# Four first chunks summed on TensorE with two products from GpSimd, one adding transfer per chunk, and a new issue order in a convolution and feed-forward kernel

## The chip, the cores and the metric

The kernel runs on one NeuronCore of one Trainium2 chip. The metric is the device time of one execution in microseconds (us), lower is better. The engines are named as in the profile: PE is TensorE (the matmuls), DVE is VectorE, ACT is ScalarE, POOL is GpSimd, and SP is SyncE, which only issues transfers.

## What is computed

For 8 sequences of 4224 positions with 192 features, each position becomes a weighted sum of itself and its six predecessors (seven taps, a softmax of given scores for each of eight heads). The result goes through a layer norm and a two-layer network with a ReLU, and is added to the network's output.

```python
w = softmax(weight_gen)                      # [8, 4224, 8 heads, 7 taps], over the taps
out = einsum('bshk,bskhg->bshg', w, x_unf)   # x_unf: the seven shifted copies of x
xn = (out - mean(out)) / sqrt(var(out) + 1e-6) * g_ln
y = out + maximum(xn @ w_ch1, 0.0) @ w_ch2   # w_ch1 [192, 768], w_ch2 [768, 192]
```

The inputs `g_ln`, `w_ch1` and `w_ch2` come as 64-bit floats, and the kernel turns them into 32-bit and then pairs of 16-bit floats itself.

## The kernel before

**Tiling.** The 33,792 positions lie as 128 partitions by 264 columns. A *chunk* is 4 or 6 columns of the convolution; a *group* is 4 columns of the network (512 positions), 66 in all. The kernel is recorded as a list of operations (`op`), and the table `PLACE` gives each a number; `order` sorts them by it, so that each engine's instruction order is written out by hand. Engines run their own lists in order and wait on semaphores.

**Convolution** (`conv`). For a chunk, four products are made: taps 1 and 2 as one pair (`c0`), taps 3 and 4 (`c1`), tap 0 alone into the chunk's output `y` (`c2`), taps 5 and 6 (`c3`). A pair goes into one `pr` buffer of two planes; there are five. For ordinary chunks DVE makes all four (line 511). Then POOL issues two transfers that add plane 2 to plane 1 and plane 4 to plane 3 (`dma_add`, line 517), and four adds on POOL (line 514) sum taps 5, 6, 1 and 3 into `y`. The first `DIRECT = 3` chunks, four columns each, go another way: POOL makes taps 5 and 6, DVE the other three products, and PE sums all seven planes into PSUM by matmuls with an identity matrix (`gather`, line 532), from where ACT copies them to `y`.

**Softmax** (`softmax`): DVE and POOL and ACT share its steps; the first transfers of scores and of `x` feed it and the first products.

**Norm** (`norm`): ACT sums and squares each column (lines 564, 569), DVE corrects the root in five small instructions (lines 597 to 603), ACT scales into `xh` (615) and rounds to 16 bits (`hl`, 635), POOL subtracts the rounded value for the low half (`lo`, 648), and SP transposes the two halves by a transfer into `xT` (`turn`, 652). Adding transfers and transposes are kept apart: each waits for the last one of the other kind that was placed ahead of it (`behind` in `order`).

**Network.** A group has three *units* of the first layer (`unit_products`, line 670, 36 matmuls each) into one of two `ph` buffers in PSUM. Each unit's result is taken out by ACT (ReLU to 16 bits, `hh`, line 685) and then by DVE (the low half, `hlo`, line 687); only then is its `ph` buffer free for the unit after next. The second layer of a group is two halves (`half_output`, `p0` and `p1`, line 721, 72 matmuls each), and DVE adds them to `y` (line 773), which SP stores (781). In the recorded loop the two halves of a group stand behind the second and third unit of the next group. `weights` prepares the weight matrices during the first 75 us; the low half of the second layer's weights (`c_w2l`, line 938, POOL) comes last. `wake` (line 642) is 11 matmuls whose result nobody reads.

Of the kernel before, what the change touches and what calls it, by code (L numbers as in the profile page):

```python
# [22 lines left out]
DIRECT = 3  # L23
# [8 lines left out]
    'wload': (3, 9, 33, 42, 82, 86, 121, 257, 191, 373, 568, 527, 770, 1053, 851, 1068, 1156, 1216, 1427, 1301,  # L32
        1465, 1705, 1809),
    'load': (26, 12, 32, 37, 85, 87, 102, 103, 84, 120, 298, 261, 337, 260, 421, 466, 456, 526, 338, 569, 642,
        641, 756, 712, 769, 783, 849, 885, 978, 1067, 979, 1162, 1159, 1163, 1302, 1343, 1368, 1369, 1572, 1426,
        1566, 1569, 1613, 1806, 1768, 1769, 1808, 1938, 1905, 2076, 2134, 2035),
    'w_load': (40, 11, 13, 0, 1, 2),
    'w_load2': (58,),
    'w_as': (67,),
    'w_av': (41, 44, 65, 73),  # L40
    'w_an': (80,),
    'w_cs': (20,),
    'w_cv': (15, 17, 22, 23),
# [223 lines left out]
def kernel(  # L267
# [735 lines left out]
```

## Time and profile before

| | |
|---|---|
| time, median of 3 runs | 868.85 us (868.65 to 870.63) |
| span of the profiled execution (first to last instruction) | 867.2 us |
| median time less that span | 1.65 us |
| PE busy | 823.4 us (95%) |
| DVE busy | 772.1 us (89%) |
| ACT busy | 683.7 us (79%) |
| POOL busy | 679.6 us (78%) |
| first unit of the network starts | 64.04 us |
| last matmul group starts | 856.81 us |

The profiled execution has no time of its own beside its span; the 1.65 us is what the time has around the span in the median of the runs. An engine's busy share is an average over stages. What matters is which engine is waited for in each stage, which the waits and the table by stage tell.

### The profile page before, as it was taken

What the parts mean: (1) busy time and instruction counts of PE and PEld (TensorE: products, weight loads), DVE (VectorE), ACT (ScalarE), POOL (GpSimd) and SP (SyncE); (2) the same over time, 40 slices, a digit from 0 to 9 for tenths busy, and PEclk for the clock granted to TensorE, in tenths of its full rate; (3) what the DMA queues carried; (4) which work ended last, traced back from release to release, by engine and by line L of the source; (5) the groups of instructions that cost most, each with busy time, mean ns of one, the idle gap of its engine ahead of it and who ended that gap; (6) DMA issues with size and microseconds to landing.
All of it is one profiled execution on the core that took longest, in us unless ns stands there. A gap on an engine that the chain in (4) does not pass through costs nothing.

```text
span 867.2 us, 37431 instructions
## 1 busy us (share of the span) xinstructions
PE 823.4 (95%) x16665; PEld 787.7 (91%) x16665; DVE 772.1 (89%) x796; ACT 683.7 (79%) x1781; POOL 679.6 (78%) x390
## 2 busy tenths in 40 slices
PE   3857999999999999999999999999999999999997
PEld 2526999999999999999999999999989999999997
DVE  6899999999999999999999999999989989874442
ACT  2798898799678889889888789787887888796631
POOL 3399999899889999897887889888976788885100
PEclk9968999999999999999999999999999999999999
DMA  7768868988897958988899698878948569565123
GB/s 193 190 127 166 166 163 184 200 176 180 194 193 151 220 94 188 213 181 180 160 205 195 149 213 175 165 139 187 207 99 200 120 151 190 124 127 106 40 76 110
DMA packets 137465, 140.89 MB, mean 162 GB/s; under 512 B 107479, under 2 KB 109015, under 8 KB 137303
## 3 DMA queue, kind: packets, MB, share of 16 engines
q1 hardware_dynamic: 123175, 88.95, 44.9%
q0 software_dynamic: 13824, 49.55, 29.6%
q8 instruction: 130, 2.13, 1.1%
q14 instruction: 32, 0.26, 0.1%
q10 hardware_dynamic: 304, 0.00, 0.0%
HBM read 36.43 MB, written 25.95 MB: 72 GB/s over the span
## 4 chain that ended last, share of the span: by engine, by line
PE 68%; DVE 9%; issue 2%; DVEq 0%
PE ph L670 34%; PE po L721 34%; DVE pr L511 4%; DVE hlo L687 2%; DVE y L511 1%; DVE y L773 1%; PE ph L750 1%; DVE sm L449 0%; DVE mx L440 0%; DVE wn L465 0%; DVE wn L460 0%; DVE wn L461 0%; DVE wn L459 0%; DVE wn L599 0%; DVE wn L601 0%
## 5 line engine op out<-in xcount | busy, mean ns | idle before, releaser
L514 POOL TENSOR_TENSOR y<-y,pr 128x1152 f32<-128x1152 f32 (+1 forms) x192 | 474.5, 2499 | 39.0 <-DVE pr L511 22.1
L670 PE MATMUL ph<-xT,c_w 64*128 64x256 f16 x7128 | 420.0, 270 | 10.5 <-DVE hlo L687 7.8
L670 PEld LDWEIGHTS <-c_w 64*128 64x128 f16 x7128 | 377.6, 94 | 28.3 <-issue 13.5
L721 PE MATMUL po<-c_w2h,hh 64*128 64x192 f16 x3120 | 392.5, 243 | 1.4 <-issue 1.0
L721 PE MATMUL po<-c_w2h,hlo 64*128 64x192 f16 x3120 | 392.4, 243 | 0.5 <-issue 0.5
L721 PE MATMUL po<-c_w2l,hh 64*128 64x192 f16 x3120 | 392.4, 243 | 0.0
L721 PEld LDWEIGHTS <-hh 64*128 64x128 f16 x6240 | 345.7, 94 | 2.8 <-issue 1.9
L511 DVE TENSOR_TENSOR pr<-x,wn 128x2304 f32<-128x2304 f32 (+1 forms) x150 | 332.5, 2226 | 6.6 <-POOL y L514 1.8
L687 DVE SCALAR_TENSOR_TENSOR hlo<-ph,hh 128x1024 f16<-128x1024 f32 x198 | 239.2, 1219 | 57.2 <-ACT hh L685 56.9
L685 ACT ACTIVATE hh<-ph 128x1024 f16<-128x1024 f32 x198 | 200.3, 1015 | 105.2 <-PE ph L670 101.7
L721 PEld LDWEIGHTS <-hlo 64*128 64x128 f16 x3120 | 225.5, 94 | 0.7 <-issue 0.7
L648 POOL TENSOR_TENSOR hl<-xh,hl 128x768 f16<-128x768 f32 x66 | 115.0, 1748 | 44.5 <-ACT hl L635 33.0
L615 ACT ACTIVATE xh<-y,s 128x192 f32<-128x192 f32 x264 | 125.5, 535 | 16.1 <-DVE s L603 12.5
L569 ACT ACTIVATE junk<-y,s 128x192 f32<-128x192 f32 x264 | 119.6, 453 | 6.9
L517 POOL DMA_DIRECT2D pr<-pr x96 | 94.4, 1082 | 37.3 <-DMA xT<-hl 14.2
L564 ACT ACTIVATE junk<-y 128x192 f32<-128x192 f32 x264 | 95.1, 360 | 13.6 <-POOL y L514 7.2
L773 DVE SCALAR_TENSOR_TENSOR y<-po,c_fs,y 128x768 f32<-128x768 f32 (+1 forms) x80 | 67.9, 860 | 5.4 <-PE po L721 5.4
L511 DVE TENSOR_TENSOR y<-x,wn 128x1152 f32<-128x1152 f32 (+1 forms) x51 | 60.0, 1181 | 0.1
L635 ACT ACTIVATE hl<-xh 128x768 f16<-128x768 f32 x66 | 55.0, 837 | 2.1 <-DMA xT<-hl 1.1
L564 ACT ACTIVATION_READ_ACCUMULATOR junk<-y 128x1 f32 x264 | 49.5, 188 | 0.0
L569 ACT ACTIVATION_READ_ACCUMULATOR junk<-y,s 128x1 f32 x264 | 49.4, 187 | 0.0
L532 PE MATMUL ph<-pr,ident 128*128 128x384 f32 x72 | 27.1, 531 | 16.5 <-DVE pr L511 15.6
(76 smaller groups left out, 298.5 us busy)
## 6 DMA issues: line engine op xcount, KB each, us to landing
pr<-pr POOLq DMA_DIRECT2D x60, 576.0 KB, 7.8
x<-in_x_dram SPq DMA_DIRECT2D x30, 576.0 KB, 6.3
out_dram<-y SPq DMA_DIRECT2D x30, 576.0 KB, 5.2
pr<-pr POOLq DMA_DIRECT2D x36, 384.0 KB, 5.8
x<-in_x_dram SPq DMA_DIRECT2D x20, 384.0 KB, 5.5
out_dram<-y SPq DMA_DIRECT2D x20, 384.0 KB, 5.3
w<-in_weight_gen_dram SPq DMA_DIRECT2D x21, 336.0 KB, 5.8
pr<-in_moe_w_ch_dram SPq DMA_DIRECT2D x1, 1152.0 KB
```

Of the source, the lines that this page charges most:

```text
L511: E.tensor_tensor(out=ov, in0=xv, in1=wv, op=ALU.mult)
L514: Q.tensor_tensor(out=flat(0), in0=flat(0), in1=flat(k), op=ALU.add)
L517: return Q.dma_start(flat(to), flat(k), accum_op=ALU.add, max_dma_last_dim=CHUNK * D * 4)
L564: A.activation(junk, at(y)[:, j, :], AF.Identity, scale=-1.0 / D, accum_out=at(s4)[:, 3, t : t + 1])
L569: A.activation(junk, at(y)[:, j, :], AF.Square, bias=at(s4)[:, 3, t : t + 1], accum_out=at(s4)[:, 0, t : t + 1])
L615: A.activation(paired(xh, t), at(y)[:, i, :].rearrange("p (c q) -> p c q", q=P // 2), AF.Identity, bias=at(s4)[:, 3, g + t : g + t + 1], s ...
L648: lambda xh=xh, hl=hl: Q.tensor_tensor(out=halves(hl, True), in0=pairs(xh), in1=halves(hl, False), op=ALU.subtract),
L670: T_.matmul(ph[:, r, v * 2 * P : (v + 1) * 2 * P], W["w1"][rows, WB[r][c], w, f : f + P], xv[rows, a, c, :, :], start=(v == 0 and k == 0), ...
L685: lambda: A.activation(at(hh)[:, us, :], at(ph), AF.Relu), [ph], [(hh, u)])
L687: lambda: V.scalar_tensor_tensor(out=at(hlo)[:, us, :], in0=at(ph), scalar=0.0, in1=at(hh)[:, us, :], op0=ALU.max, op1=ALU.subtract),
L721: made.append(T_.matmul(at(po)[:, z, e * D : (e + 1) * D], token(b, 2 * z + e, j)[rows], W[w][rows, j, :], start=(ph == 0 and e == 0 and k ...
L773: V.scalar_tensor_tensor(out=ysl, in0=at(po)[:, zs[0] : zs[-1] + 1, : 2 * D], scalar=W["fs"][:, 0:1], in1=ysl, op0=ALU.mult, op1=ALU.add)
```

## The change

The first part of four columns is cut into two chunks of two columns, and `DIRECT` is 4, so the same first twelve columns are summed by PE, as four chunks of 2, 2, 4 and 4 columns. For these chunks POOL makes taps 3 and 4 too (`BY_POOL = (3, 5)`). The five two-plane buffers `pr` are replaced by two four-plane buffers `pq` (taps 1 to 4) and two two-plane buffers `pr` (taps 5 and 6). The two adding transfers of an ordinary chunk become one, which adds planes 2 and 4 to planes 1 and 3 when both are there. The helper buffer of the weight preparation moves from `pr` to `xh`. In the recorded loop the second group's three units all stand ahead of the first group's two output halves. And `PLACE` is new as a whole.

```diff
-DIRECT = 3
+DIRECT = 4
+BY_POOL = (3, 5)
...
-    'unit': (209, 210, 224, 228, 232, 249, 264, 279, 288, 302, 304, 328, 341, 342, 369, 379, 388, 406, 423, 426,
+    'unit': (162, 171, 193, 219, 229, 237, 268, 270, 291, 306, 307, 325, 343, 349, 364, 388, 393, 408, 422,
...
-    'p0': (248, 287, 327, 368, 405, 448, 481, 503, 554, 588, 636, 670, 703, 723, 771, 807, 839, 870, 905, 948,
+    'p0': (244, 278, 316, 351, 397, 432, 469, 510, 546, 584, 619, 656, 697, 720, 755, 791, 821, 857, 893,
...
-    pool("pr", 5, [P, 2, CHUNK, D], F32)
+    pool("pq", 2, [P, 4, CHUNK, D], F32)
+    pool("pr", 2, [P, 2, CHUNK, D], F32)
...
-            m = min(CHUNK, n - o) if n % CHUNK == 0 else min(4, n - o)
+            m = 2 if s0 == 0 else min(CHUNK, n - o) if n % CHUNK == 0 else min(4, n - o)
...
-        prs = {k: Buf("pr") for k in (1, 3, 5)}
+        pq, pr = Buf("pq"), Buf("pr")
...
+        def plane(k, nk=1):
+            b, i = (pq, k - 1) if k < 5 else (pr, k - 5)
+            return at(b)[:, i : i + nk, :n, :]
...
-        def dma_add(to, k):
-            return Q.dma_start(flat(to), flat(k), accum_op=ALU.add, max_dma_last_dim=CHUNK * D * 4)
+        def dma_add():
+            a = at(pq).rearrange("p (i j) t d -> p j i (t d)", j=2)[:, :, :, : n * D]
+            return Q.dma_start(a[:, 0], a[:, 1], accum_op=ALU.add, max_dma_last_dim=CHUNK * D * 4)
...
-            if direct and i == 3:
-                op("Pool", q_ns(2 * nd), (f"c{i}", t0), lambda k=k: mul(k, 2, Q), [*xr, (ch["soft"]["e"], "w")], w)
+            if direct and k in BY_POOL:
+                op("Pool", 1.89 * 2 * nd, (f"c{i}", t0), lambda k=k: mul(k, 2, Q), [*xr, (ch["soft"]["e"], "w")], w)
...
-        for i, k in enumerate((1, 3)):
-            op("Pool", 610, (f"d{i}", t0), lambda k=k: dma_add(k, k + 1), [(prs[k], 1)],
-               [(prs[k], 0)], dma=600.0 + 400.0 * n, kind="add")
+        op("Pool", 610, ("d0", t0), dma_add, [tap(2), tap(4)], [tap(1), tap(3)], dma=600.0 + 800.0 * n, kind="add")
...
-        m, t = Buf("pr"), Buf(space)
+        m, t = Buf("xh"), Buf(space)
...
+            late = prev["prev"] is not None and prev["prev"]["prev"] is None
             for u in range(3):
                 products(prev, u)
-                if u and prev["prev"]:
+                if u and prev["prev"] and not late:
                     half_output(prev["prev"], u - 1, prev["s"])
+            if late:
+                for z in range(2):
+                    half_output(prev["prev"], z, prev["s"])
```

The first numbers of `unit` and `p0` show the order on PE: before, five units (209 to 232) stand ahead of the first `p0` (248); now six (162 to 237) stand ahead of it (244).

On DVE, at the first products of the direct chunks (line 511 before, 521 now; `x` times the softmax weights `wn`), before:

```order
L511 TENSOR_TENSOR pr1_77<-x_63,wn0_104 128x2x768
L511 TENSOR_TENSOR y0_67<-x_63,wn0_104 128x768
L459 TENSOR_SCALAR wn0_104<-sm1_97 128x64
L460 TENSOR_TENSOR wn0_104<-wn0_104,rr1_95 128x64
L461 SCALAR_TENSOR_TENSOR wn0_104<-wn0_104,rr1_95 128x64
L511 TENSOR_TENSOR pr2_78<-x_63,wn0_104 128x2x768
L465 TENSOR_TENSOR wn0_104<-e1_99,wn0_104 128x448
L440 TENSOR_REDUCE mx0_92<-w2_66 128x96
L511 TENSOR_TENSOR pr3_79<-x_63,wn0_104 128x2x768
L511 TENSOR_TENSOR y1_68<-x_63,wn0_104 128x768
L511 TENSOR_TENSOR y2_69<-x_63,wn0_104 128x768
L511 TENSOR_TENSOR pr4_80<-x_63,wn0_104 128x2x768
```

and now:

```order
L521 TENSOR_TENSOR pq0_76<-x_63,wn0_103 128x2x384
L462 TENSOR_SCALAR wn0_103<-sm1_96 128x64
L463 TENSOR_TENSOR wn0_103<-wn0_103,rr1_94 128x64
L464 SCALAR_TENSOR_TENSOR wn0_103<-wn0_103,rr1_94 128x64
L847 SCALAR_TENSOR_TENSOR ph0_104<-hh0_87,ph0_104 128x384
L521 TENSOR_TENSOR y0_67<-x_63,wn0_103 128x384
L521 TENSOR_TENSOR pq1_77<-x_63,wn0_103 128x2x384
L850 SCALAR_TENSOR_TENSOR ph0_104<-hh0_87,ph0_104 128x384
L521 TENSOR_TENSOR y1_68<-x_63,wn0_103 128x384
L854 SCALAR_TENSOR_TENSOR hlo0_89<-xh0_80,ph0_104 128x384
L468 TENSOR_TENSOR wn0_103<-e1_98,wn0_103 128x448
L443 TENSOR_REDUCE mx0_91<-w2_66 128x96
```

A direct chunk has one pair product on DVE now instead of two, and the first two chunks have half-size ones; the softmax and weight steps between them stay.

On POOL at the start (442 before and 445 now are the softmax's subtraction, 517 and 528 the adding transfer, 905 and 913 the first layer's low weights, 648 and 656 `lo`), before:

```order
L511 TENSOR_TENSOR pr0_76<-x_63,e0_98 128x2x768
L442 TENSOR_TENSOR e0_98<-w2_66,mx0_92 128x672
L511 TENSOR_TENSOR pr2_78<-x_63,e1_99 128x2x768
L511 TENSOR_TENSOR pr4_80<-x_63,e1_99 128x2x768
L442 TENSOR_TENSOR e0_98<-w0_64,mx1_93 128x672
L442 TENSOR_TENSOR e1_99<-w1_65,mx0_92 128x672
L517 DMA pr3_79<-pr3_79 128x768
L648 TENSOR_TENSOR hl0_83<-xh0_81,hl0_83 128x2x384
```

and now:

```order
L521 TENSOR_TENSOR pr1_79<-x_63,e0_97 128x2x384
L445 TENSOR_TENSOR e0_97<-w2_66,mx0_91 128x672
L521 TENSOR_TENSOR pq0_76<-x_63,e1_98 128x2x768
L521 TENSOR_TENSOR pr0_78<-x_63,e1_98 128x2x768
L445 TENSOR_TENSOR e0_97<-w1_65,mx1_92 128x672
L521 TENSOR_TENSOR pq1_77<-x_63,e1_98 128x2x768
L521 TENSOR_TENSOR pr0_78<-x_63,e1_98 128x2x768
L528 DMA pq0_76<-pq0_76 128x2x768
L445 TENSOR_TENSOR e1_98<-w0_64,mx0_91 128x672
L913 TENSOR_TENSOR c_w1_126<-hlo0_89,c_w1_126 128x768
L913 TENSOR_TENSOR c_w1_126<-hlo0_89,c_w1_126 128x384
L656 TENSOR_TENSOR hl0_82<-xh0_80,hl0_82 128x2x384
```

Three more half-size products stand just ahead of this piece, so POOL makes four products of each size where it made three of full size, and one adding transfer is issued ahead of the first `lo`.

On DVE around the first evictions of the network (`hlo`, line 687 before, 695 now), from the first to the fourth before:

```order
L687 SCALAR_TENSOR_TENSOR hlo0_90<-ph1_106,hh0_88 128x1024
L459 TENSOR_SCALAR wn0_104<-sm0_96 128x96
L460 TENSOR_TENSOR wn0_104<-wn0_104,rr0_94 128x96
L461 SCALAR_TENSOR_TENSOR wn0_104<-wn0_104,rr0_94 128x96
L687 SCALAR_TENSOR_TENSOR hlo0_90<-ph0_105,hh0_88 128x1024
L511 TENSOR_TENSOR pr3_79<-x_63,wn0_104 128x2x768
L687 SCALAR_TENSOR_TENSOR hlo0_90<-ph1_106,hh0_88 128x1024
L440 TENSOR_REDUCE mx1_93<-w1_65 128x96
L511 TENSOR_TENSOR pr1_77<-x_63,wn0_104 128x2x768
L687 SCALAR_TENSOR_TENSOR hlo1_91<-ph0_105,hh1_89 128x1024
```

and from the second to the fourth now:

```order
L695 SCALAR_TENSOR_TENSOR hlo0_89<-ph0_104,hh0_87 128x1024
L521 TENSOR_TENSOR y7_74<-x_63,wn0_103 128x768
L521 TENSOR_TENSOR y8_75<-x_63,wn0_103 128x768
L462 TENSOR_SCALAR wn0_103<-sm0_95 128x96
L463 TENSOR_TENSOR wn0_103<-wn0_103,rr0_93 128x96
L464 SCALAR_TENSOR_TENSOR wn0_103<-wn0_103,rr0_93 128x96
L695 SCALAR_TENSOR_TENSOR hlo0_89<-ph1_105,hh0_87 128x1024
L521 TENSOR_TENSOR pr0_78<-x_63,wn0_103 128x2x768
L695 SCALAR_TENSOR_TENSOR hlo1_90<-ph0_104,hh1_88 128x1024
```

The evictions follow closer on each other. Counted over both orders from the start, what stands ahead of the fourth eviction is five pair products of 1536 elements, two reduces of the softmax and one five-instruction root correction fewer, and two products of 384 elements more.

## Rows read from the trace of the kernel before

**Rows 1.** The page's first part: busy time of each engine, share of the span, and count of instructions.

```profile
PE 823.4 (95%) x16665; PEld 787.7 (91%) x16665; DVE 772.1 (89%) x796; ACT 683.7 (79%) x1781; POOL 679.6 (78%) x390
```

**Rows 2.** The table by stage, four stretches and two finer ones of the start: stretch in us, its length, then busy us and instructions of PE, PEld, DVE, ACT and POOL, the granted clock of PE, the DMA engines' share and GB/s.

```profile
0.00:80.00 80.00, 47.38 (x255) 29.25 (x257) 67.15 (x112) 54.51 (x150) 51.36 (x39) 0.87 0.73 168
80.00:270.00 190.00, 187.38 (x3976) 186.26 (x3972) 187.39 (x195) 160.97 (x436) 174.65 (x113) 1.00 0.84 182
270.00:856.00 586.00, 581.81 (x12360) 565.68 (x12356) 515.19 (x488) 468.21 (x1196) 453.63 (x240) 1.00 0.74 156
...
0.00:20.00 20.00, 6.33 (x11) 3.53 (x12) 12.84 (x25) 4.79 (x12) 7.50 (x11) 1.00 0.77 197
20.00:40.00 20.00, 17.13 (x55) 9.94 (x55) 16.96 (x28) 14.46 (x46) 5.90 (x3) 1.00 0.81 212
70.00:80.00 10.00, 6.34 (x78) 5.31 (x79) 8.32 (x11) 7.43 (x13) 10.00 (x7) 0.66 0.79 156
```

**Rows 3.** The waits of PE from 80 to 270 us and then from 270 to 856 us: who waited for whom, us in total, times, longest.

```profile
PE ph L670 <- DVE hlo L687: 2.6, 6, 1.0
PE po L721 <- DVE y L773: 0.3, 1, 0.3
...
PE ph L670 <- issue: 2.5, 2, 1.4
PE po L721 <- issue: 1.5, 2, 1.0
```

**Rows 4.** The waits of DVE from 0 to 80 us, same columns.

```profile
DVE mx L440 <- DMA w<-in_weight_gen_dram: 2.9, 2, 2.5
DVE pr L511 <- DMA x<-in_x_dram: 1.8, 1, 1.8
DVE hlo L687 <- ACT hh L685: 1.6, 1, 1.6
DVE pr L511 <- PE po L860: 1.4, 1, 1.4
DVE pr L511 <- ACT e L471: 1.1, 1, 1.1
```

**Rows 5.** PE in order of time at the start of the network: start, us, instruction and count, and the idle time before with what ended it.

```profile
59.45 4.66 PE L642 MATMUL ph<-hl 128*128 128x512 f16 x11
64.04 4.10 PE L670 MATMUL ph<-xT,c_w 64*128 64x256 f16 x72
73.35 6.08 PE L670 MATMUL ph<-xT,c_w 64*128 64x256 f16 x72 [5.21 <-DVE hlo L687]
79.75 2.14 PE L670 MATMUL ph<-xT,c_w 64*128 64x256 f16 x36 [0.31 <-DVE hlo L687]
81.71 0.26 PE L721 MATMUL po<-c_w2h,hh 64*128 64x192 f16 x2
```

**Rows 6.** DVE in order of time, single lines of it: three pair products in a row and the next instruction; then a reduce and its successor; and the fourth eviction.

```profile
60.69 5.07 DVE L511 TENSOR_TENSOR pr<-x,wn 128x1536 f32<-128x1536 f32 x3
65.68 0.15 DVE L863 TENSOR_SCALAR c_r<-po 128x1 f32<-128x1 f32 x1
...
68.74 0.17 DVE L597 TENSOR_SCALAR wn<-s 128x4 f32<-128x4 f32 x1
...
69.49 2.67 DVE L511 TENSOR_TENSOR y<-x,wn 128x768 f32<-128x768 f32 x3
...
79.61 0.84 DVE L440 TENSOR_REDUCE mx<-w 128x96 f32<-128x672 f32 x1
80.37 1.75 DVE L511 TENSOR_TENSOR pr<-x,wn 128x1536 f32<-128x1536 f32 x1
82.03 1.22 DVE L687 SCALAR_TENSOR_TENSOR hlo<-ph,hh 128x1024 f16<-128x1024 f32 x1
```

**Rows 7.** Groups by line, kept apart by form, over the whole span: shapes, count, busy us and mean ns of one, idle time before and its releasers.

```profile
L511 DVE TENSOR_TENSOR pr<-x,wn 128x1536 f32<-128x1536 f32 x60 | 104.1, 1746 | 6.0 <-DMA x<-in_x_dram 1.8 <-POOL y L514 1.6 <-PE po L860 1.4
L773 DVE SCALAR_TENSOR_TENSOR y<-po,c_fs,y 128x768 f32<-128x768 f32 x50 | 50.5, 1010 | 3.4 <-PE po L721 3.4
L511 DVE TENSOR_TENSOR y<-x,wn 128x768 f32<-128x768 f32 x21 | 19.6, 946 | 0.0
L773 DVE SCALAR_TENSOR_TENSOR y<-po,c_fs,y 128x384 f32<-128x384 f32 x30 | 17.4, 610 | 2.0 <-PE po L721 2.0
L511 POOL TENSOR_TENSOR pr<-x,e 128x1536 f32<-128x1536 f32 x3 | 8.7, 2904 | 17.5 <-ACT e L471 7.2 <-ACT pr L849 6.0 <-DMA x<-in_x_dram 4.3
L517 POOL DMA_DIRECT2D pr<-pr x96 | 94.4, 1082 | 37.3 <-DMA xT<-hl 14.2 <-DVE pr L511 10.3 <-DVE hlo L687 7.5
```

**Rows 8.** One period of the steady part, from the chain that ended last: start, us, what.

```profile
709.72 1.97 PE ph L670 x36
711.69 2.97 PE po L721 x72
714.66 3.93 PE ph L670 x72
718.59 2.97 PE po L721 x72
721.56 0.47 PE ph L670 x9
```

**Rows 9.** Adding transfers and transposes: the instructions that issue two adding transfers of 576 KB from 332.2 to 333.5 us, with the least, median and greatest time from issue to landing of the two; the same last line for all 66 transposes; and SP's waits over the whole span for the transposes (line 652).

```profile
L517 POOL DMA_DIRECT2D pr<-pr x2: 869/1024/1180, 332.4 to 332.9; - x2
...
DMA to landing us min/median/max: 7.9/9.2/10.5
...
DMA to landing us min/median/max: 3.2/3.7/7.2
...
SPq L652 <- DMA pr<-pr: 166.0, 30, 11.2
```

**Rows 10.** POOL in order of time around the first `lo` and SP's first transposes.

```profile
44.79 1.94 POOL L648 TENSOR_TENSOR hl<-xh,hl 128x768 f16<-128x768 f32 x1
...
56.39 1.60 SPq L652 DMA_TRANSPOSE xT<-hl  x1
```

More of the change, by code (lines that the diff above doesn't have):

```diff
@@ new lines @@
+    'w_load': (16, 2, 0, 32, 28, 24),
+    'w_load2': (72,),
+    'w_as': (88,),
+    'w_av': (76, 82, 86, 94),
+    'w_an': (95,),
+    'w_cs': (45,),
+    'w_cv': (18, 33, 39, 46),
+    'w_cn': (60,),
+    'w_s1': (103, 104, 109, 110, 115),
+    'w_h': (120, 126, 124, 132),
+    'w_l': (129, 135),
+    'w_m': (139, 136, 145, 142),
+    'w_c2s': (105, 160, 181),
+    'w_c2v': (113, 118, 119, 123, 127, 130, 155, 164, 172, 178, 182, 187),
+    'w_c2n': (151, 186, 191),
+    'w_s2': (203, 206, 208, 211, 213, 214, 217, 225),
@@ new lines @@
+    'max': (6, 12, 51, 84, 98, 125, 269, 391, 355, 488, 732, 663, 949, 1118, 861, 1184, 1317, 1291, 1506,
+        1437, 1542, 1710, 1787),
+    'sub': (8, 15, 52, 85, 121, 235, 331, 430, 565, 669, 745, 883, 952, 1126, 1051, 1220, 1338, 1406, 1527,
+        1653, 1781, 1819, 1973),
+    'exp': (11, 20, 56, 92, 153, 248, 378, 442, 604, 676, 777, 894, 1052, 1159, 1060, 1253, 1352, 1412,
+        1552, 1659, 1814, 1843, 1987),
+    'sum': (14, 22, 61, 143, 179, 271, 450, 475, 616, 694, 826, 924, 1072, 1183, 1088, 1282, 1431, 1446,
+        1599, 1799, 1832, 1926, 2083),
@@ new lines @@
+    'rcp': (17, 26, 64, 168, 210, 304, 467, 495, 653, 714, 849, 955, 1101, 1185, 1099, 1306, 1436, 1485,
+        1607, 1803, 1880, 1948, 2089),
+    'inv': (19, 29, 66, 207, 222, 407, 505, 611, 712, 768, 864, 1009, 1115, 1197, 1285, 1339, 1475, 1613,
+        1639, 1808, 1897, 1998, 2103),
+    'mul': (21, 48, 79, 212, 322, 425, 536, 642, 735, 824, 923, 1014, 1119, 1211, 1314, 1401, 1521, 1617,
+        1707, 1809, 1905, 2002, 2106),
+    'keep': (23, 49),
[16 rows of a table added]
+    'copy': (65, 73, 111, 146),
+    'sums': (69, 75, 117, 112, 169, 148, 200, 205, 242, 263, 276, 257, 299, 292, 344, 334, 399, 386, 421,
[7 rows of a table added]
@@ L492, in conv, with tap @@
         yw = [(y, j) for j in range(n)]
+        def plane(k, nk=1):
+            b, i = (pq, k - 1) if k < 5 else (pr, k - 5)
+            return at(b)[:, i : i + nk, :n, :]
+        def tap(k):
+            return (pq, k) if k < 5 else (pr, k)
         def flat(k):
@@ L535, in conv @@
             for i, ks in enumerate(((1, 2), (0,), (3, 4), (5, 6))):
[L536 to L537 removed]
+                op("PE", 160 * n * len(ks), (f"z{i}", t0), lambda ks=ks, i=i: gather(ks, i == 0, i == 3),
+                   [q for k in ks for q in ([tap(k)] if k else yw)], [z], lat=400.0)
             op("ACT", a_ns(nd, 150), ("copy", t0),
@@ L825, in mv @@
         def mv():
-            return at(m)[rows, 0].rearrange("p t d -> p (t d)")[:, :n]
+            return at(m)[rows].rearrange("p t d -> p (t d)")[:, :n]
         def tv(dt):
```

76 lines of the change are left out of this document (20 added, 56 removed), and 235 rows, old and new, of the table PLACE.

## The prediction

> **What bounds the kernel now.** I read the busy shares first: PE leads with 823.4 of 867.2 us, DVE follows with 772.1 [rows 1]. A share mixes stages, so the table by stage comes next [rows 2]. It shows three. Up to 80 us the network barely runs and nothing is full: PE 47.4, DVE 67.2 and POOL 51.4 of 80 us. From 80 to 270 us PE and DVE are both full, 187.38 and 187.39 of 190. From 270 to 856 us PE is full (581.8 of 586) and DVE has room (515.2). The waits say who holds whom [rows 3]: from 80 to 270 us PE waits for DVE alone (evictions of the first layer 2.6 us, an output 0.3); after 270 us it waits for no engine and no transfer, only 4.0 us in four pauses that the profile ascribes to nothing. So from 270 us on the kernel is a fixed amount of matmul work, 11.84 us for each group of four columns (one period: 709.72 to 721.56) [rows 8], and the end moves by what PE is ahead or behind at about 270 us. Until then DVE decides, so the time is won or lost before 80 us, in what DVE has done by then.
>
> **DVE's work: what goes.** The direct chunks lose their taps 3 and 4 on DVE. Before, three chunks of four columns had six pair products of 1536 elements; now two chunks of four have two, and the two of two columns have one half-size pair each (768 elements). A product of 1536 costs 1.746 us, one of 768 0.946 [rows 7]; one of 384 I estimate from these at 0.5. So four of 1536 go (-6.98), two of 768 come and one tap-0 product of 768 goes (+0.95), two tap-0 products of 384 come (+1.0). The first group's output is added in two pieces, since it lies in two `y` buffers: 2 x 0.610 for 1.010 [rows 7], +0.21. Sum: -4.8 us, all of it ahead of 80 us except the last term.
>
> **DVE's idle time.** DVE idles 80 - 67.15 = 12.85 us before 80 us [rows 2]. The waits name some of it [rows 4]: 2.9 for the first scores, 1.8 for the first `x`, 1.6 for an eviction behind ACT, 1.4 behind PE and 1.1 behind ACT. The scores stay first in need and nothing there gets shorter. The first `x` transfer shrinks from 1920 to 1536 elements a partition, and the sums on PE come in smaller pieces, sooner. The last four can win between 0 and 5.9 us; new waits can cost: a chunk's taps 1 to 4 now need one of only two `pq` buffers. A loss as large as the work saved, 4.8, is where I put that end. I take -2.5, a little under half of the 5.9, since each of the four stands before work that the new order brings forward. DVE is then 4.8 + 2.5 = 7.3 us ahead.
>
> **PE's start.** Five units ran before the first output half, which started at 81.71 [rows 5]; the sixth needs the fourth eviction, since there are two `ph` buffers. That eviction started at 82.03 [rows 6]. Ahead of it the new order has five products of 1536 less (start to start (65.68 - 60.69) / 3 = 1.66 each), two reduces less (80.37 - 79.61 = 0.76), one root correction less (69.49 - 68.74 = 0.75) and two products of 384 more (about 0.5): -8.3 - 1.5 - 0.75 + 1.0 = -9.6 [rows 6]. With 2.5 less idle it starts at 82.03 - 9.6 - 2.5 = 69.9 and ends 1.22 later; the sixth unit runs 1.97 [rows 6, 8] to 73.1, and the first half follows. The same six units would have been done at 81.71 + 1.97 = 83.7 before. PE is 10.5 us ahead at that point, more than DVE. In the stretch up to 270 us, where PE waits for DVE, that shrinks towards DVE's 7.3.
>
> **What POOL gets.** Before, three products of 1536 elements at 2.904 us [rows 7]; now four of 768 and four of 1536, together 9216 elements for 4608, so 17.4 us for 8.7. POOL was busy 7.50 + 5.90 of the first 40 us [rows 2], so 26.6 us are free to take 8.7 more. The deadline is the first `lo`: it stood at 44.79 and its transpose left only at 56.39 [rows 10]. The new order puts the first layer's low weights and one adding transfer ahead of it, and even 9 us later it would be no later than the transpose was. I cost it at nothing; if POOL's free time is not where the products are ready, each us beyond that margin is a us on the first unit, not yet on the sixth.
>
> [...]
>
> **Adding transfers.** 96 issues at about 1 us of POOL [rows 7] become 48. POOL is not waited for by PE anywhere [rows 3], so this earns nothing directly. The bytes are the same. A merged transfer of 1152 KB is not in the trace; the nearest rows are a single one of 576 KB (7.9 us to landing) and two issued 0.5 apart, of which the second landed at 332.9 + 10.5 = 343.4, 11.0 after the first issue [rows 9]. I take 11.0, as the same bytes go through the same queue, and keep 7.9 for the lower end.
>
> **The sum.** Against the profiled span: 867.2 - 7.3 = 859.9. With the 1.65 us that the median has around the span: **861.5 us**, 0.8% less than 868.85. PE's work is unchanged: the four direct chunks hold as many columns as the three did.
>
> **Rivals.**
> *PE keeps its lead.* If DVE's order lets PE run through, the gain is 10.5: 858.4. For it: DVE has more to spare in the later groups, and the last long DVE wait was under 1.0 us [rows 3]. Against it: DVE at 187.39 of 190 us [rows 2] cannot catch up 3 us there. What PE's clock does to it: after an idle stretch of 5.21 us the next 72 matmuls took 6.08 for 4.10 before it, at a granted 0.66 in that stretch [rows 2, 5]. PE has three idle stretches now before the first half (ahead of the first, third and fourth unit) for one. [...]
> [...]
>
> *The saved work is idled away.* The two `pq` buffers make DVE wait for PE's sums at the start, or the longer ACT queue ahead of the first ReLUs does. It decides if DVE's idle before 80 us rises by 4.8 or so, to 17.6: then 868.9, no change. For it: the direct chunks pass through two buffers for taps 1 to 4 where they had a choice of five smaller ones. Against it: four chunks are summed on PE with no other matmuls between them.
>
> *The merged transfer holds up the transposes: slower.* Transposes wait for the last adding transfer ahead of them, 30 times and 166 us in total before [rows 9], behind which no PE wait stood [rows 3]. An ordinary chunk of six columns has 1.5 x 11.84 = 17.8 us [rows 8]. Its merged transfer (11.0), one and a half transposes (3.7 each, 5.6) and two hand-overs make about 17, so it fits by less than 1 us. If the merged transfer lands after 13.0 instead of 11.0 on the mean, because loads and stores share the 16 DMA engines, a chunk takes 18.8, 1.0 too long, over the 30 chunks of six columns: +30, less 7.3, gives 891. It decides from about 11.9 us on. Against it: the two adding transfers of a chunk could already stand back to back, as in these rows, so the phases of the two kinds grow little, and before 856 us no unit from 80 us on waited for `xT` [rows 3].
>
> *It does not do what it says* would show as unchanged transfers; the order on POOL shows 48, so no chance is kept for it.
>
> **How the numbers follow.** The forecast (DVE's lead decides, with idle from -5 to +2, so 859 to 866) gets 0.62; PE keeping its lead (858.4 to 860.4) 0.16; the saved work idled away (866.3 to 871.4) 0.11; slower by transfers 0.11. Under about 0.3% (2.6 us) a measurement of this kernel does not tell from no change. So faster 0.78, same 0.11, slower 0.11. The range from 857.0 to 868.5 holds the first two cases and about half of the third's lower part; it leaves out the slower case and a part of the third.
>
> **What would show it.** In the profile after: DVE busy about 767 in all, 4.8 less; DVE idle before 80 us near 10; the first output half of PE near 73 with six units ahead of it; from there to 270 us PE's waits for evictions at least as long as the 2.6 of before, and none after 270; POOL's adding transfers 48, landing in about 11 us for six columns. Wrong would be: PE waiting for the transposed tiles in the steady part (then the transfers decide), DVE idle of 17 us or more by 80 us, or a lead at 270 us that is kept below 4 or above 9.

## The result, and the profile after

The changed kernel takes 880.22 us in the median (874.97 to 882.24, four runs), the kernel before beside it 869.68. The ratio is 1.012, with a 95% interval from 1.0085 to 1.0155: 1.2% slower, where 0.8% faster was forecast. The profiled execution is the fastest of the four (874.97, span 872.8), so what it shows of the loss is the lower end: 5.6 us of span, where the medians differ by 10.5. About half of the loss, then, stands in no profile.

The page's first part of the changed kernel, busy time of each engine (against [rows 1]):

```profile
PE 826.9 (95%) x16693; PEld 801.4 (92%) x16693; DVE 768.5 (88%) x796; ACT 682.6 (78%) x1782; POOL 662.7 (76%) x347
```

The table by stage, same columns as [rows 2]:

```profile
0.00:80.00 80.00, 57.32 (x517) 45.79 (x519) 70.16 (x115) 60.44 (x169) 65.74 (x46) 0.91 0.83 195
80.00:270.00 190.00, 185.36 (x3906) 179.13 (x3904) 185.96 (x199) 161.10 (x426) 164.51 (x94) 1.00 0.84 175
270.00:856.00 586.00, 571.57 (x12067) 564.27 (x12063) 506.83 (x479) 459.45 (x1188) 432.47 (x209) 1.00 0.78 156
```

DVE has 3.6 us less work, and idles 80 - 70.16 = 9.84 us before 80 us instead of 12.85. The start went as forecast. But PE, full after 270 us before (581.81 of 586), is now idle there for 14.4 us.

PE in order of time at the start of the network in the changed kernel (against [rows 5]):

```profile
46.05 5.77 PE L678 MATMUL ph<-xT,c_w 64*128 64x256 f16 x72 [1.99 <-DMA xT<-hl]
55.72 3.29 PE L678 MATMUL ph<-xT,c_w 64*128 64x256 f16 x36 [3.90 <-DVE hlo L695]
...
63.94 3.50 PE L678 MATMUL ph<-xT,c_w 64*128 64x256 f16 x36 [3.56 <-DVE hlo L695]
67.75 2.14 PE L678 MATMUL ph<-xT,c_w 64*128 64x256 f16 x36 [0.31 <-DVE hlo L695]
70.55 2.14 PE L678 MATMUL ph<-xT,c_w 64*128 64x256 f16 x36 [0.66 <-DVE hlo L695]
72.51 0.26 PE L729 MATMUL po<-c_w2h,hh 64*128 64x192 f16 x2
```

Six units (72 + 4 x 36 matmuls) stand ahead of the first output half, which starts at 72.51; forecast was 73. The same work would have been done at 83.7 before, so PE is 11.2 us ahead there (forecast 10.5).

How much of that is left where DVE stops deciding? The 52nd unit tells, the first of group 17 (counted from 0). PE in order of time, the kernel before (the view ends 12 matmuls into the unit):

```profile
270.86 0.83 PE L670 MATMUL ph<-xT,c_w 64*128 64x256 f16 x12
```

and the changed kernel:

```profile
263.03 4.11 PE L678 MATMUL ph<-xT,c_w 64*128 64x256 f16 x72
```

7.8 us ahead, forecast 7.3. From there to the end 7.8 + 5.6 = 13.4 us are lost. The waits of PE in the changed kernel, from 80 to 270 us and from 270 to 856 us (against [rows 3]):

```profile
PE ph L678 <- DMA xT<-hl: 2.9, 2, 2.6
PE ph L678 <- DVE hlo L695: 0.7, 1, 0.7
...
PE ph L678 <- issue: 6.9, 4, 2.7
PE po L729 <- issue: 4.4, 4, 2.3
PE ph L678 <- DMA xT<-hl: 2.7, 2, 2.4
```

Two things are new. PE waits for transposed tiles (5.6 us in all), which it never did after 80 us before. And the pauses that the profile ascribes to nothing, 4.0 us before, are 11.3. What are they? One of them in order of time:

```profile
519.42 0.27 PE L678 MATMUL ph<-xT,c_w 64*128 64x256 f16 x1
521.72 0.50 PE L678 MATMUL ph<-xT,c_w 64*128 64x256 f16 x6 [2.03 <-issue]
```

The DMA queues of the changed kernel in the 7.7 us ahead of it (511.7 to 519.4) and, for comparison, from 499.4 to 507.4 us (queue, packets, MB, share of the 16 engines):

```profile
q0 software_dynamic: 200, 0.92, 73.5%
q1 hardware_dynamic: 160, 0.67, 31.2%
...
q1 hardware_dynamic: 1480, 0.92, 50.2%
q0 software_dynamic: 154, 0.71, 48.9%
q8 instruction: 1, 0.02, 1.0%
```

The third queue, "instruction", is the key: the page counts 130 packets of it with 2.13 MB, so 16 KB each, one per 257 of PE's 2 x 16,693 instructions (a weight load for each matmul); no other engine has more than 1782 instructions there, so by the count they are taken for PE's. Between 80 and 850 us they begin 6.2 us apart in the mean. In the 7.7 us ahead of the pause there is none. By the times of the packets in the trace, one began at 510.63 and the next only at 519.44, and PE went on 2.3 us after that. All eight pauses after 270 us of the changed kernel are of this kind, and the four of the kernel before as well: the last instruction packet ahead of PE's going on came 6.7 to 11.2 us after the one before it, and PE went on 2.2 to 2.8 us after that packet began (once 4.0). A long spacing alone makes no pause: of the 125 spacings between 80 and 850 us in the changed kernel 50 are 6.7 us or more. A pause of the kernel before in order of time:

```profile
634.46 0.61 PE L670 MATMUL ph<-xT,c_w 64*128 64x256 f16 x7 [1.39 <-issue]
```

and its DMA queues from 624.5 to 632.0 us:

```profile
q0 software_dynamic: 247, 0.99, 68.8%
q1 hardware_dynamic: 142, 0.59, 22.8%
```

No instruction packet either. Where the pauses stand says the same without the queues. The table by stage of the changed kernel from the start up to two of them (at 445.98 and 453.58; the counts behind the busy times of PE and PEld are the matmuls and weight loads done):

```profile
0.00:445.95 445.95, 414.07 (x8030) 390.69 (x8031) 426.12 (x471) 371.12 (x989) 375.67 (x208) 0.98 0.85 178
0.00:453.56 453.56, 420.49 (x8158) 396.94 (x8159) 433.62 (x479) 376.00 (x998) 383.12 (x211) 0.98 0.85 178
```

128 matmuls and 128 weight loads lie between them, 256 instructions, about one packet by the page (257). All twelve pauses stand after a multiple of 128 matmuls and 94 more: 34, 60, 62, 63, 74, 75, 86 and 99 times 128 in the changed kernel, 57, 64, 92 and 98 times in the kernel before. So PE stops each time at the same place in a stretch of 256 instructions. That a packet ends there is read from the 257, not shown by itself.

So the 11.3 us of pauses that the view puts down to nothing are read here as waits for PE's own instructions. The page counts their packets on the same 16 DMA engines as the queue of the adding transfers, with 1.0% of the engines' time for 31.6%.

After one of the eight pauses PE also ran slower, the one at 530.40 (2.28 us), 8.7 us after the one at 521.72. The table by stage of the changed kernel around it:

```profile
530.00:535.00 5.00, 4.60 (x60) 4.59 (x61) 0.52 (x1) 0.40 (x3) 4.48 (x2) 0.66 1.11 247
```

The granted clock is 0.66 in the mean: by finer windows 1.00 up to 530.5 us, 0.50 from 531.0 to 534.0 and 1.00 again from 534.5, which makes 3.4 us at 0.50 and 1.7 us lost. It is the only such stretch between 90 and 856 us; in the rest the granted clock is 1.00. Of the 13.4 us, then, 11.3 - 4.0 = 7.3 are late instructions, 2.7 transposed tiles and 1.7 the clock after that pause. Of the 1.7 left only 0.2 are shorter gaps; the rest is time in which the view has PE busy, and stays unexplained.

### The profile page after: what moved, and what is told of

It is laid out like the page before. It is cut to its first block, busy times and chain, and to the rows that moved or that the text cites. A ratio compares the mean times of both kernels' runs of the same rounds, so it can differ in the third digit from the quotient of the medians.

```text
span 872.8 us, 37365 instructions
## 1 busy us (share of the span) xinstructions
PE 826.9 (95%) x16693; PEld 801.4 (92%) x16693; DVE 768.5 (88%) x796; ACT 682.6 (78%) x1782; POOL 662.7 (76%) x347
## 3 DMA queue, kind: packets, MB, share of 16 engines
q0 software_dynamic: 13056, 49.55, 31.6%
q8 instruction: 130, 2.13, 1.0%
## 4 chain that ended last, share of the span: by engine, by line
PE 73%; DVE 10%; DMA 5%; POOL 5%; ACT 4%; issue 3%; SPq 1%; DVEq 0%; POOLq 0%; ACTq 0%
PE ph L678 37%; PE po L729 36%; POOL y L524 3%; DVE pq L521 3%; DMA xT<-hl 2%; DVE hlo L695 2%; DMA hh<-in_moe_w_ch_dram 1%; DVE pr L521 1%; DVE y L521 1%; ACT xh L623 1%; DMA pq<-pq 1%; POOL hl L656 1%; PE ph L758 1%; DVE y L781 1%; DMA x<-in_x_dram 1%
## 5 line engine op out<-in xcount | busy, mean ns | idle before, releaser
L678 PE MATMUL ph<-xT,c_w 64*128 64x256 f16 x7128 | 425.1, 271 | 24.2 <-DVE hlo L695 9.1
L678 PEld LDWEIGHTS <-c_w 64*128 64x128 f16 x7128 | 387.5, 95 | 37.4 <-issue 22.0
L729 PEld LDWEIGHTS <-hh 64*128 64x128 f16 x6240 | 354.8, 94 | 3.7 <-issue 2.2
L524 POOL TENSOR_TENSOR y<-y,pr 128x1152 f32<-128x1152 f32 (+1 forms) x96 | 238.0, 2489 | 18.5 <-DVE pr L521 10.5
L524 POOL TENSOR_TENSOR y<-y,pq 128x1152 f32<-128x1152 f32 (+1 forms) x96 | 230.3, 2399 | 24.5 <-DMA pq<-pq 20.7
L729 PEld LDWEIGHTS <-hlo 64*128 64x128 f16 x3120 | 233.1, 94 | 4.6 <-issue 4.5
L521 DVE TENSOR_TENSOR pq<-x,wn 128x2304 f32<-128x2304 f32 (+2 forms) x100 | 220.0, 2209 | 2.3 <-DMA x<-in_x_dram 1.9
L528 POOL DMA_DIRECT2D pq<-pq x48 | 57.6, 1219 | 69.3 <-DMA xT<-hl 29.8
L521 DVE TENSOR_TENSOR pr<-x,wn 128x2304 f32<-128x2304 f32 (+1 forms) x48 | 107.7, 2244 | 0.4 <-PE ph L543 0.4
L521 DVE TENSOR_TENSOR y<-x,wn 128x1152 f32<-128x1152 f32 (+2 forms) x52 | 60.0, 1161 | 0.5 <-DMA out_dram<-y 0.3
```

What stands on the lines that cost most here:

```text
L521: E.tensor_tensor(out=ov, in0=xv, in1=wv, op=ALU.mult)
L524: Q.tensor_tensor(out=flat(0), in0=flat(0), in1=flat(k), op=ALU.add)
L528: return Q.dma_start(a[:, 0], a[:, 1], accum_op=ALU.add, max_dma_last_dim=CHUNK * D * 4)
L678: T_.matmul(ph[:, r, v * 2 * P : (v + 1) * 2 * P], W["w1"][rows, WB[r][c], w, f : f + P], xv[rows, a, c, :, :], start=(v == 0 and k == 0), ...
L729: made.append(T_.matmul(at(po)[:, z, e * D : (e + 1) * D], token(b, 2 * z + e, j)[rows], W[w][rows, j, :], start=(ph == 0 and e == 0 and k ...
```

## The experiments

Fifteen runs of fourteen kernels. Each ratio is against runs of the kernel before on the same chip, which took 868.26 to 869.68 us there; a difference of two rows of other chips carries up to 1.4 us of that besides the intervals.

| kernel | median us | ratio (95%) |
|---|---|---|
| changed kernel | 880.22 | 1.012 (1.0085 to 1.0155) |
| e1, e9: two transfers back to back | 871.93 | 1.0035 (1.0015 to 1.0055) |
| e2: before, transfers merged | 963.3 | 1.1102 (1.1085 to 1.1119) |
| e3: changed, adding cut to a column | 861.02 | 0.9916 (0.9903 to 0.9929) |
| e4: changed, taps 3 and 4 on DVE | 886.2 | 1.0178 (1.0142 to 1.0213) |
| e5: before, adding cut to a column | 866.29 | 0.9972 (0.9961 to 0.9984) |
| e6: two transfers, rows halved | 880.63 | 1.0143 (1.0122 to 1.0165) |
| e7: two transfers, the first early | 877.14 | 1.0095 (1.0076 to 1.0113) |
| e8: changed, stores cut to a column | 869.5 | 1.0014 (0.9997 to 1.0031) |
| e10: new start, old order from 115 us | 859.67 | 0.9899 (0.988 to 0.9917) |
| e11: e10 with loads beside adding | 862.8 | 0.9933 (0.991 to 0.9956) |
| e12: e1 with loads away from adding | 875.55 | 1.0068 (1.0044 to 1.0093) |
| e13: old order from 275 us | 860.73 | 0.9909 (0.9887 to 0.993) |
| e14: old order from 374 us | 863.95 | 0.9947 (0.993 to 0.9964) |
| e15: old order from 545 us | 868.52 | 1.0003 (0.9978 to 1.0028) |

### Is it the merged transfer? (e1, e9, e2)

```diff
-        op("Pool", 610, ("d0", t0), dma_add, [tap(2), tap(4)], [tap(1), tap(3)], ...)
+        for i, k in enumerate((1, 3)):
+            op("Pool", 610, (f"d{i}", t0), lambda k=k: dma_add(k), [tap(k + 1)], [tap(k)], ...)
```

> The changed kernel with its one adding transfer of 1152 KB per chunk cut back into two of 576 KB, issued one after the other at the same place; nothing else differs. In the profile of the changed kernel PE is 7.8 us ahead of before at the 52nd unit (263.03 for 270.86), as forecast, and loses 13.5 us afterwards: pauses ascribed to nothing (11.3 us after 270 us, 4.0 before), at each of which a 16 KB packet of the instruction queue had been late, and 5.6 us of waits for transposed tiles. Theory 1, the merged transfer is the cause (its packets stand in one lump in front of the instruction packets and of the transposes): the pauses fall back to about 4 us, the waits for transposed tiles under 1 us, time 860 to 865. Theory 2, the new order is the cause (where adding transfers, loads and stores meet): the lumps stay as large, two transfers back to back carry the same bytes, time 875 to 882 as the changed kernel.

871.93, between the two theories: 3.4 us above the kernel before instead of 10.5, so the split brings back 7 us (8.3 between the medians of the two rows). A profile of the same kernel:

> One more profile of the changed kernel with two adding transfers per chunk back to back (871.9 in the median before). If the merging's part of the loss is the late instruction packets, PE's pauses ascribed to nothing come out at 4 to 7 us for the changed kernel's 11.6, and what is still lost against the 861.0 without most of the adding (some 11 us) stands as waits for transposed tiles, for evictions and at the lower clock. Rival: pauses as in the changed kernel, 10 us or more, and the gain was elsewhere.

PE's waits in it from 80 to 270 and from 270 to 856 us (span 871.7):

```profile
PE ph L679 <- DMA xT<-hl: 4.0, 3, 2.9
PE ph L679 <- DVE hlo L696: 1.0, 2, 0.7
...
PE ph L679 <- issue: 4.2, 4, 2.3
PE po L730 <- issue: 2.7, 3, 1.8
PE ph L679 <- DMA xT<-hl: 1.6, 3, 1.2
```

The pauses fall from 11.3 to 6.9, the waits for transposed tiles stay at 5.6. From the 52nd unit to the end of the span this profile takes 605.5 us for the 609.8 of the changed kernel: 4.3 less, about what the pauses gave back. So after 270 us the merging works through the late instructions, as far as one profile of each can show. Ahead of that unit, which starts at 266.22 for 263.03, it had lost 3.2 us more, so that the two spans are only 1.1 us apart; the 7 to 8 us of the merging rest on the times alone.

The merging alone, in the order of before, was to show the other half:

```diff
+            i, j = sorted((prs[1].slot, prs[3].slot))
+            a = PR[:, i : j + 1 : j - i, :, :n, :].rearrange("p i j t d -> p j i (t d)")
+            return Q.dma_start(a[:, 0], a[:, 1], accum_op=ALU.add, ...)
```

> The kernel before, in its own order, with the two adding transfers of a chunk merged into one, issued where the later of the two stood (45 of the 48 chunks; the three others, where the first sum is needed before the second transfer, keep two). Theory 1, the merged transfer is the cause: pauses of PE ascribed to nothing rise from 4 to 9 us or more, waits for transposed tiles appear, time 874 to 882. Theory 2, the new order is the cause: pauses stay near 4 us, time 867 to 871.

It missed both: 963.3. DVE's waits from 80 to 960 us tell why:

```profile
DVE pr L508 <- DMA pr<-pr: 38.1, 5, 14.4
...
DVE pr L508 <- POOL y L511: 13.7, 8, 3.6
```

In that order the five two-plane buffers are handed on after the first of two transfers; merged, they come free later and DVE stands. The run prices that, not the merging, and settles nothing here.

### What do the adding transfers cost in either order? (e3, e5)

```diff
-            a = at(pq).rearrange(...)[:, :, :, : n * D]
+            a = at(pq).rearrange(...)[:, :, :, :D]
```

> The changed kernel with the same 48 adding transfers at the same places, but each adds only the first column of its chunk (192 KB for 1152 or 768), so most of the sums of taps 2 and 4 are left out. Theories 1 and 2 (PE's instruction packets and the transposes are late because of the adding transfers' bytes): pauses under 2 us, no waits for transposed tiles after 80 us, the lead of 7.3 to 8 us at 270 us kept or larger, time 857 to 861. Rival (the pauses have nothing to do with the transfers, but with the order of instructions on PE or with loads and stores): pauses of 8 us or more, time 870 to 880.

861.02, at the upper end of what was expected. PE's waits from 270 to 856 us:

```profile
PE ph L678 <- DMA xT<-hl: 1.4, 3, 0.5
PE ph L678 <- issue: 1.3, 1, 1.3
PE po L729 <- issue: 0.7, 1, 0.7
```

With the bytes most of the pauses go (2.0 us are left of 11.3), and a time like the forecast appears. The same cut in the kernel before:

> The kernel before, its 96 adding transfers cut to the first column of each chunk (96 KB for 576 or 384), so most of the sums of taps 2 and 4 are left out; its order is untouched. It prices the adding transfers in the old order; in the changed kernel they cost 19 us (880.2 for 861.0), split in two 11 (871.9 for 861.0). Theory 1, the new order and the merging make the transfers dear and the old order hid them: only the 4.0 us of pauses and some first-layer waits go, 863 to 866. Theory 2, they cost about the same in every order and the 7.8 us of lead at 270 us is not worth anything: 858 to 861, no slower than the changed kernel with the same cut.

866.29, just above the 863 to 866 of the first theory: the adding transfers cost 2 us in the kernel before (868.26 beside this run) and 18 to 19 in the changed one (18 against the kernel before beside each run, 19 between the medians). The start is worth 866.29 - 861.02 = 5.3 us with most of the adding bytes cut.

### Does DVE's work decide the lead? (e4)

```diff
-BY_POOL = (3, 5)
+BY_POOL = (5,)
```

In the order one of the moved products goes a few places earlier (78 for 90).

> The changed kernel with taps 3 and 4 of the four direct chunks back on DVE (two products of 768 elements, 0.946 each, and two of 1536, 1.746 each: 5.4 us more work for DVE before 80 us). If DVE decides PE's lead, as forecast, the 52nd unit starts 4 to 6 us later than in the changed kernel, at 267 to 269 for 263.03. Rival (PE's early start decides and DVE had room): 263 to 265. What is lost after 270 us should be as in the changed kernel, 8 to 15 us, so 878 to 888 by the first and 874 to 883 by the second.

The first unit of group 17:

```profile
266.83 4.11 PE L678 MATMUL ph<-xT,c_w 64*128 64x256 f16 x72
```

3.8 us later than in the changed kernel, just under the 4 to 6 expected. The median is 6.0 us higher, though the two intervals overlap. 5.4 us of work on DVE took 3.8 of lead: DVE decides, with some slack.

### Which property of the transfers? (e6, e7, e8)

> The changed kernel with two adding transfers per chunk (as in the run of that kind, 871.9) whose rows are cut in two (2304 bytes at most for 4608): same bytes, same issues, twice the rows. If an instruction packet gets its turn between two rows, its wait shrinks and the pauses with it: 865 to 869. If it waits for the bytes that are queued ahead of it, nothing changes: 870 to 874. If shorter rows move slower, later transposes: over 875.

880.63, 8.7 more than with whole rows: pauses of 5.3 us, but more waits of other kinds. Shorter rows are no remedy.

> The changed kernel with two adding transfers per chunk, the first of which is issued as soon as its own pair of products is made and the transposes ahead have had time to land, some 1 to 7 us ahead of the second, in 44 of 48 chunks. If it is the lump that delays PE's instruction packets and the transposes (bytes that stand in front at one moment), two half lumps apart cost less than back to back: 862 to 868. If the sum of bytes decides, 870 to 874 as back to back; if POOL, which waits for the transposes at each adding transfer, is held up, more than 874.

877.14, 5.2 more than back to back. PE's waits from 270 to 856 us:

```profile
PE ph L677 <- DVE hlo L694: 4.5, 3, 3.5
PE ph L677 <- issue: 3.9, 3, 2.3
PE ph L677 <- DMA xT<-hl: 1.9, 4, 0.7
PE po L728 <- issue: 1.8, 3, 1.3
```

The pauses are a little shorter again (5.7), but evictions are late. A likely reason, not tested by itself: POOL stands 25.3 us for transposes ahead of adding transfers between 80 and 870 us, 18.5 back to back.

> The changed kernel, merged transfers as they are, but each store of the output writes only the first column of its range (so the rest of the output is left out): some 20 of 141 MB fewer, none of them in the queue of the adding transfers. If the fill of the shared DMA engines delays the instruction packets and the transposes, whoever fills them, 862 to 870. If only the adding transfers' own size does, 874 to 881 as the changed kernel.

869.5: 10.7 us come back between the medians (9.3 against the kernel before) though the adding transfers are whole. PE's waits from 270 to 856 us:

```profile
PE ph L678 <- DMA xT<-hl: 5.6, 6, 1.9
PE ph L678 <- issue: 4.4, 5, 1.4
PE po L729 <- issue: 1.1, 2, 0.8
```

The pauses halve (5.5 for 11.3), the waits for tiles do not fall (5.6 for 2.7). So here the bytes of another queue lengthen the pauses too, and not the adding transfers' own size alone. It also means that these prices do not add up: 18 to 19 us for the adding and some 10 for the stores are more than the 10.5 us lost.

### Where in the new order? (e10 to e15)

e10 takes the changed kernel up to place 380 of its table, and gives every operation behind it the place that it has in the old table (a direct chunk shifts the count by one), with two transfers per chunk in six two-plane buffers.

> The changed kernel's start joined to the order of before: four direct chunks, taps 3 to 6 of them on POOL, six units ahead of the first output half, new order up to its place 380 (to about 115 us), from there on every remaining operation in the relative order of the kernel before, with its two separate adding transfers per chunk (six two-plane buffers). If the new order of the later part and the merging eat the lead, as the runs so far say (the adding transfers cost 2 us in the old order, 866.3 for 868.3, and 19 in the new), the lead is kept but for what the adding costs there: 862 to 865. Rival, the lead itself makes the transfers late, since PE needs its transposed tiles 5 to 7 us sooner: 867 to 872.

859.67, below the 862 to 865 expected, and the fastest kernel of this study. The first unit of its group 17:

```profile
263.74 4.11 PE L680 MATMUL ph<-xT,c_w 64*128 64x256 f16 x72
```

and PE's waits from 80 to 270 and from 270 to 856 us:

```profile
PE po L731 <- DVE y L783: 3.3, 2, 2.9
PE ph L680 <- DVE hlo L697: 1.8, 4, 0.7
PE ph L680 <- DMA xT<-hl: 0.2, 1, 0.2
...
PE po L731 <- issue: 1.6, 2, 1.4
PE po L731 <- SPq L741: 0.2, 1, 0.2
```

7.1 us ahead, and no transposed tile is late by more than 0.2 us: here the lead itself does not make transfers late. The later part of the new order does, together with its buffers, which e10 changes as well.

e11 and e12 move only loads on SP, in e10 to beside the adding transfers, in e1 away from them.

> The joined kernel (new start, old order behind, 859.7) with 30 of its loads of x and of scores moved on SP from between the transposes to right behind the next adding transfer; same instructions, same bytes, nothing else reordered. Counted from issue to landing in the traces between 120 and 800 us, two or more loads or stores are in flight beside an adding transfer for 5.3% of the time in the kernel before and 6.4 in the joined one, but 10.5 in the changed kernel and 11.7 with its transfers split. Theory, this coincidence makes PE's instruction packets and the transposes late: the share rises to 10% or more, the pauses from 1.6 to 5 us or more, 864 to 870. Rival, something else in the new order costs the 12 us between 871.9 and 859.7: 858 to 862.

862.8: the share of time with two loads or stores beside an adding transfer rose from 6.4 to 10.2% as meant, yet this cost 3.1 us, with intervals that just overlap, and not the 4 to 10 of the theory, and the pauses stayed at 1.7 us.

> The changed kernel with two adding transfers per chunk (871.9), with 12 of its loads of x moved on SP from beside an adding transfer to right behind the next transpose; same instructions and bytes. By the same theory the share of two or more loads or stores beside an adding transfer falls from 11.7 to some 9%, and the time by a third or so of the 12 us: 866 to 869. Rival: 870 to 874, no change.

875.55, no faster than e1 (the intervals overlap), where the theory had 866 to 869. No profile of it at such a time was kept, so it is not shown that the share fell as meant. By e11, where the share did rise, the theory explains some 3 of the 12 us.

Then the new order was kept for longer, in three steps.

> The joined kernel with the new order kept for 18 groups (54 units, to about 275 us) instead of 5 (15 units, to about 115). Theory, few crowded places of the new order cost it: in the profile of the split kernel two waits for transposed tiles at 120 and 158 us take 2.5 us of lead that the joined kernel keeps, so 861 to 864. Rival, the loss is spread evenly over the new order, 12 us in 740: some 2.6 for these 160 us, 861 to 864 too, told apart only by the next two. Rival, the new order up to here is harmless: 858 to 861.

> As before, new order for 26 groups, to about 374 us. Few crowded places: the split kernel loses little between 275 and 374 us, so within 1.5 us of the cut at 275. Spread evenly: 1.6 us more than there.

> As before, new order for 40 groups, to about 545 us, and so with the place at 490 to 531 us where the profiles of the changed and of the split kernel show two adding transfers, two stores and up to four loads in flight at a time and two pauses of 2 us each with a stretch at the lower clock. Few crowded places: 5 to 8 us above the cut at 374, 868 to 872. Spread evenly: 2.8 us above it.

859.7, 860.7, 864.0, 868.5 with the cut at 115, 275, 374 and 545 us, and 871.9 with the new order to the end (in the buffers of the changed kernel). Of 12.2 us, 1.1 come with the new order up to 275 (the intervals of e10 and e13 overlap, so it may be harmless there), 3.2 and 4.6 with the next two stretches, 3.4 with the rest and its buffers. The stretch to 374 cost more than either theory had (3.2), that to 545 nearly what crowded places had (4.6 for 5 to 8). Two places of the cut at 545 in PE's order of time:

```profile
119.08 5.77 PE L680 MATMUL ph<-xT,c_w 64*128 64x256 f16 x72 [2.82 <-DMA xT<-hl]
...
524.12 5.75 PE L680 MATMUL ph<-xT,c_w 64*128 64x256 f16 x71 [2.84 <-issue]
```

The same wait for a tile near 119 us and the same pause near 522 us stand in the changed kernel (118.70 and 521.72), in e9 (119.82 and 525.00) and, the first, in the cut at 374 (118.66). The pause comes after the same 9566 matmuls in all three. In two of these kernels, e9 and e15, the next two units also run longer after each of them, 5.5 to 5.8 us for 4.1; around the pause of e15 the granted clock is 0.83 in the mean from 520 to 530 us, and 1.00 from 500 to 510.

The wait, though, does not follow from the order alone. Up to 270 us the cuts at 275, 374 and 545 run the same operations in the same order on every engine, and in the profile of the cut at 275 the same two units run without it:

```profile
115.39 4.10 PE L680 MATMUL ph<-xT,c_w 64*128 64x256 f16 x72
```

There the 52nd unit starts at 261.05, in the cut at 374 at 264.51. That is 3.5 of the 4.2 us by which the spans of these two profiles differ (858.8 and 863.0), and it stands ahead of the place where their orders part. So the steps tell what keeping the new order longer costs, not where in the run it is lost.

## Why the prediction was wrong

**What held.** DVE's work fell by 3.6 us (forecast 4.8), its idle time by 3.0 (2.5). The first output half stood at 72.51 (73). At 270 us the lead was 7.8 (7.3), but luck has a part in that. The sum cut PE's first lead by waits for DVE's evictions; these were 0.7 us from 80 to 270 us, and 2.9 went to transposed tiles, which the sum did not have. In e3, where no tile was late before 270 us, the evictions took 2.9 us and the 52nd unit started at 261.79, a lead of 9.1. POOL took its extra products without delay: the first unit starts at 46.05 for 64.04, and with taps 3 and 4 back on DVE (e4) the lead is 3.8 us smaller and the median 6.0 higher, though a product of 1536 elements takes POOL 2.904 us and DVE 1.746, 1.66 times as long [rows 7]. Without most of the adding the kernel takes 861.02, and with the old order behind the new start 859.67, for the forecast 861.5; these are other kernels, and show what the start can be worth, not that the sum was right.

**The step that failed** is the one on adding transfers: that one transfer instead of two has the same bytes and "earns nothing directly", and, under it, the reading that from 270 us on the kernel is a fixed amount of matmul work because PE "waits for no engine and no transfer". The 4.0 us of pauses "that the profile ascribes to nothing" were taken as no wait at all. By the packets' times they were waits for PE's own instructions. They hang on the data transfers: without most of the adding bytes 1.7 us are left of them in the kernel before (e5) and 2.0 in the changed one (e3), and the transfers and the order of the changed kernel lengthened them. After 270 us PE stood for 14.4 us instead of 4.2, 11.3 of it for instructions and 2.7 for transposed tiles. So the transfers and their order in the later part had a price, and the sum put it at nothing: no term asked what the new order does after 270 us.

**The rivals.** The third, that merged transfers hold up the transposes, had the right direction and part of the culprit at a chance of 0.11, but the size was wrong, and waits for tiles were the smaller part of the loss. Its point of decision was a landing after 11.9 us on the mean. The changed kernel's page:

```profile
pq<-pq POOLq DMA_DIRECT2D x30, 1152.0 KB, 9.8
```

9.8 in the median and 10.6 in the mean of the 30, below the 11.0 taken, so by its own rule it should not have decided, and 891 did not come. The second rival fell: DVE's idle time shrank. The first, PE keeping its whole lead, fell as well, 11.2 becoming 7.8 by 270 us. The other end of its range, 860.4, takes the sixth unit 2.0 us longer at a lower clock, and no run shows that. In the changed kernel the granted clock was 0.63 in the third unit (3.29 us) and 0.59 in the fourth (3.50), but 1.00 in the sixth, which took 2.14 us as the fifth did.

**The signs.** "Waits for evictions at least as long as 2.6" between 80 and 270 us was wrong (0.7): the wait for tiles near 119 us (2.56 us) had already taken that time from PE. "None after 270" held for evictions, and said nothing of the 14.4 us that PE stood for other things. "PE waiting for the transposed tiles in the steady part" was named as a sign of being wrong, and it came.

**What is shown and what stays open.** Shown: without the bytes of the adding transfers the loss is gone (e3), and without those of the stores nearly so (e8), so it is what the transfers do together. Between the medians, 8.3 us go with the merging (e1) and 12.2 with the order after 115 us and its buffers (e10, e13 to e15), the two together more than the loss because the start gains. That the pauses are late instruction packets is read from the packets' times and from PE's count of instructions in twelve cases of two kernels; no run moved the packets by themselves. Open: which rule makes one order crowd and another not, and what the executions near the median lose beyond the profiled one. Loads beside adding transfers were tried and are not enough.

## What to carry to other kernels

A pause on TensorE that the profile ascribes to nothing is to be looked up in two places. In the DMA queues, here, an instruction packet had begun 2 to 4 us ahead of the end of the pause and the one before it 6.7 us or more earlier; in the counts of matmuls, the pauses stood whole multiples of 128 apart. Both held in all twelve pauses here, and with the edit that merged and reordered the transfers the pauses went from 4.0 to 11.3 us. A lead won early is only kept if the rest of the order can hold it, so price the order of the later part as its own term, and test a new start with the old order behind it. To price a kind of transfer, cut its bytes in both kernels: here 2 us before and 18 to 19 after said in two runs where the gain had gone. Cut a second kind as well before calling the first the cause: the stores gave back most of the loss too.

## What the hardware showed that was not expected

- The instruction queue moved 130 packets of 16 KB, one per 257 of TensorE's instructions, on the same 16 DMA engines as the data (1.0% of their time), and all twelve pauses stand whole multiples of 256 instructions apart, counted from the start. At these pauses, of up to 2.74 us and at one time two within 9 us, the packet had come 6.7 to 11.2 us after the one before it (6.2 in the mean in the changed kernel).
- One adding transfer of 1152 KB lands after 9.8 us in the median. Two of 576 KB back to back (e9) have both landed 9.1 us after the first issue, by the trace's issue and landing times. The difference is small, and yet the merged kernel takes 7 to 8 us longer.
- Rows of 2304 bytes instead of 4608 in the adding transfers cost 8.7 us (e6 for e1), though the landing time of one hardly changed (8.2 for 7.9 us).
